# A mixture of experts with 608 static slots an expert in place of 640

## The chip, the core and the metric

The kernel runs on one core of a Trainium2 chip, in one launch. The time is the device time of that core in microseconds (us), from the start to the end of the program. Beside the timed runs one execution was taken by the hardware profiler; every duration in this document comes from that execution. TensorE (PE) multiplies, and its weight loads are recorded apart (PEld) because they run beside the products; VectorE (DVE), ScalarE (ACT) and GpSimd (POOL) do the elementwise work, and SyncE's queue (SP) issues most DMAs.

## What is computed

Attention with only the 32 largest scores of each row kept, then a feed-forward layer with a squared ReLU, then a mixture of eight experts of which each token uses two. Cut to the part that matters here:

```python
def _moe2_ref(x, w_gate, w_noise, noise, w1, w2):        # x: 2304 tokens of 512
    noisy_logits = x @ w_gate + np.log1p(np.exp(x @ w_noise)) * noise
    top2 = np.argpartition(-noisy_logits, 2, axis=1)[:, :2]
    top2_w = softmax of the two logits
    for e in range(8):
        for k in range(2):
            mask = top2[:, k] == e
            h = np.maximum(x[mask] @ w1[e], 0.0)          # 512 -> 1024
            out[mask] += top2_w[mask, k, None] * (h @ w2[e])
```

2304 tokens with two choices each make 4608 rows over eight experts, 576 on average. How many an expert gets depends on the data.

## The kernel before

Attention runs first, with the feed-forward layer and the routing of finished tokens as background work. The routing writes each token's row, with its two gate weights, its first expert and its token number in four more columns (`ROW` = 516), into the DRAM buffer `xs`, in which expert e owns the rows from e x 2304 on; `base` counts how many it has. The first `CAP` = 640 rows of each expert are its static slots: they have been filled with empty rows (`zero_fill`, by tiles of 128), and the code for them is laid out without a look at the counts. Rows beyond them go through a general path at the end (`over`, `extra`, `blank`, `beyond`), under a branch that is taken only when some expert has more than `CAP` rows.

The 640 slots are five tiles of 128, in two parts: columns 0 to 384 (three tiles) and 384 to 640 (two tiles), `PARTS`. `fetch` (L507) loads a tile of rows (`mr`, L514), turns it by four transposes on TensorE (L517) into a PSUM tile `ph`, and splits it into a high part on ACT (L521) and a low part on DVE (L522), both fp32r, `xe`; `gate` works out the gate weight and the token number on POOL (`info`).

`expert` (L529) first gathers the current output rows (`cur`, L539, an indirect DMA). Then it goes over eight blocks f of 128 hidden units. A block loads its weights (`raww`, L559, three buffers), splits them into high and low on ACT (L563) and DVE (L564) as `wi` and `wo`, and for each part makes 12 products into `ph` (L570 to L572: four slices of the 512 inputs, high x high, high x low, low x high), with the part's columns moving. ReLU (ACT, L576) and the low rest (DVE, L577) give `ht`. One block later `second` makes three products a tile (L551 to L553) with 128 columns of `ht` as weights and the 512 columns of `wo` moving, and adds over the blocks in the tile's bank `acc` (three banks, two more named `acc2`). After the last block DVE makes `y` = `acc` x gate + `cur` (L591, three buffers) and POOL writes it by token number (L592, an indirect DMA).

The first parts of experts 0 and 1 (`EARLY`) run earlier, beside the last feed-forward work; their second parts follow alone, and then experts 2 to 7 with both parts. While an expert runs, the next one's tiles are fetched, one a block. `ph` has two buffers, so a block's first product waits until DVE has read the block before last. The order on each engine comes from a scheduler that goes by priorities and by modelled times; nothing of it is written by hand.

Of the kernel before, what the change touches and what calls it, by code (L numbers as in the profile page):

```python
# [8 lines left out]
F32 = mybir.dt.float32  # L9
F32R = mybir.dt.float32r  # L10
I32 = mybir.dt.int32
# [3 lines left out]
ALU = mybir.AluOpType  # L15
PSUM = bass.MemoryType.PSUM

P = 128
# [34 lines left out]
def attention_ffn_moe(ctx: ExitStack, tc: tile.TileContext, q, k, v, w_ffn, w_route, noise, w_exp, out,  # L53
# [3 lines left out]
    nc = tc.nc  # L57
    B, H, S, D = SHAPE
    NT, DM = out.shape
# [4 lines left out]
    NFE = F // P  # L64
    NC = DM // P
# [3 lines left out]
    SCALE = 1.0 / float(D) ** 0.5  # L69
    CH = 384  # L70
    CT = CH // P
    CAP = 640
    CAPT = CAP // P
    PARTS = [(0, 384), (384, CAP - 384)]
    ROW = DM + 4

# [3 lines left out]
    xs = nc.dram_tensor(f"xs{tag}", (E * NT, ROW), F32, kind="Internal").ap()  # L80
# [3 lines left out]
    ident = cpool.tile([P, P], F32, name="ident")  # L84
# [19 lines left out]
    for t, (b, i) in enumerate(tiles):  # L104
        if i == 0:
            nc.gpsimd.iota(tok_i[:, t:t + NFULL], pattern=[[P, NFULL]], base=b * S, channel_multiplier=1)
        elif i is None:
            nc.gpsimd.iota(tok_i[:, t:t + 1], pattern=[[0, 1]], base=b * S + NFULL * P, channel_multiplier=1)
            nc.gpsimd.tensor_scalar(tok_i[LEFT:P, t:t + 1], tok_i[LEFT:P, t:t + 1], 1.0, float(S - LEFT),
                                    op0=ALU.mult, op1=ALU.add)  # L110
# [387 lines left out]
    def gate(gi, xr, e):  # L498
        nc.gpsimd.tensor_scalar(gi[:, 0:1], xr[:, DM + 2:DM + 3], float(e), xr[:, DM:DM + 1],  # L499
                                op0=ALU.is_equal, op1=ALU.mult)  # L500
        nc.gpsimd.tensor_scalar(gi[:, 1:2], xr[:, DM + 2:DM + 3], float(e), None, op0=ALU.is_equal)  # L501
        nc.gpsimd.tensor_scalar(gi[:, 1:2], gi[:, 1:2], -1.0, 1.0, op0=ALU.mult, op1=ALU.add)
        nc.gpsimd.tensor_tensor(gi[:, 1:2], gi[:, 1:2], xr[:, DM + 1:DM + 2], op=ALU.mult)
        nc.gpsimd.tensor_tensor(gi[:, 2:3], gi[:, 0:1], gi[:, 1:2], op=ALU.add)
        nc.gpsimd.tensor_copy(gi[:, 3:4].bitcast(I32), xr[:, DM + 3:DM + 4].bitcast(I32))

    def fetch(e, parts):  # L507

        xe = [mpool.tile([P, 2, NC, n], F32R, name=f"xe{o}") for o, n in parts]
        t0, t1 = parts[0][0] // P, sum(parts[-1]) // P  # L510
        info = mpool.tile([P, CAPT, 4], F32, name="info")
        for t in range(t0, t1):
            xr = mpool.tile([P, ROW], F32, name="mr", bufs=3)
            nc.sync.dma_start(xr, xs[e * NT + t * P:e * NT + (t + 1) * P, :])  # L514
            pt = ps_m.tile([P, DM], F32, name="ph")
            for c in range(NC):
                nc.tensor.transpose(pt[:, c * P:(c + 1) * P], xr[:, c * P:(c + 1) * P], ident)  # L517
            i, off = place(parts, t)
            hi, lo = xe[i][:, 0, :, off:off + P], xe[i][:, 1, :, off:off + P]
            pv = pt.rearrange("p (c s) -> p c s", c=NC)  # L520
            nc.scalar.activation(hi, pv, AF.Copy)  # L521
            nc.vector.tensor_tensor(lo, pv, hi.bitcast(F32), op=ALU.subtract)  # L522
            gate(info[:, t, :], xr, e)
            yield None
        yield xe, info

# [2 lines left out]
    def expert(e, parts, ahead):  # L529

        xe, info = found.pop(0)
        tiles_ = range(parts[0][0] // P, sum(parts[-1]) // P)
        cur = {}
        for t in tiles_:
            cu = cur[t] = mpool.tile([P, DM], F32, name="cur", bufs=6)
            if cleared[0] < 6:
                nc.gpsimd.memset(cu, 0.0)
                cleared[0] += 1
            nc.gpsimd.indirect_dma_start(  # L539
                out=cu, out_offset=None, in_=out,  # L540
                in_offset=bass.IndirectOffsetOnAxis(ap=info[:, t, 3:4].bitcast(I32), axis=0),
                bounds_check=NT - 1, oob_is_err=False)
        acc = {}
        for n, t in enumerate(tiles_):
            acc[t] = ps_acc.tile([P, DM], F32, name="acc") if n < 3 else ps_m.tile([P, DM], F32, name="acc2")

        def second(f, wo, hs):
            for t in tiles_:
                i, off = place(parts, t)
                sl = slice(off, off + P)  # L550
                nc.tensor.matmul(acc[t], hs[i][:, 0, sl], wo[:, 0, :], start=(f == 0), stop=False)  # L551
                nc.tensor.matmul(acc[t], hs[i][:, 0, sl], wo[:, 1, :], start=False, stop=False)  # L552
                nc.tensor.matmul(acc[t], hs[i][:, 1, sl], wo[:, 0, :], start=False, stop=(f == NFE - 1))  # L553
                yield True, 0.5

        prev = None
        for f in range(NFE):
            raw = mpool.tile([P, 2, DM], F32, name="raww", bufs=3)
            nc.sync.dma_start(raw, w_exp[e, f])  # L559
            wi = fpool.tile([P, 2, DM], F32R, name="wi", bufs=2)  # L560
            wo = fpool.tile([P, 2, DM], F32R, name="wo", bufs=2)
            for i, w in enumerate((wi, wo)):
                nc.scalar.activation(w[:, 0, :], raw[:, i, :], AF.Copy)  # L563
                nc.vector.tensor_tensor(w[:, 1, :], raw[:, i, :], w[:, 0, :].bitcast(F32), op=ALU.subtract)  # L564
            hs = []
            for i, (o, n) in enumerate(parts):
                ph = ps_m.tile([P, DM], F32, name="ph")
                for c in range(NC):
                    sl = slice(c * P, (c + 1) * P)
                    nc.tensor.matmul(ph[:, 0:n], wi[:, 0, sl], xe[i][:, 0, c, :], start=(c == 0), stop=False)  # L570
                    nc.tensor.matmul(ph[:, 0:n], wi[:, 0, sl], xe[i][:, 1, c, :], start=False, stop=False)  # L571
                    nc.tensor.matmul(ph[:, 0:n], wi[:, 1, sl], xe[i][:, 0, c, :], start=False, stop=(c == NC - 1))  # L572
                    if c < NC - 1:
                        yield True, 0.5
                ht = mpool.tile([P, 2, n], F32R, name=f"ht{o}")
                nc.scalar.activation(ht[:, 0, :], ph[:, 0:n], AF.Relu)  # L576
                nc.vector.scalar_tensor_tensor(ht[:, 1, :], ph[:, 0:n], 0.0, ht[:, 0, :].bitcast(F32),  # L577
                                               op0=ALU.max, op1=ALU.subtract)
                hs.append(ht)
                yield True, 0.5  # L580
            if prev is not None:
                yield from second(*prev)
            prev = (f, wo, hs)
            if f >= 1:
                x = next(ahead, None)
                if x is not None:
                    found.append(x)
        yield from second(*prev)
        for t in tiles_:
            y = mpool.tile([P, DM], F32, name="y", bufs=3)  # L590
            nc.vector.scalar_tensor_tensor(y, acc[t], info[:, t, 2:3], cur[t], op0=ALU.mult, op1=ALU.add)  # L591
            apart(row_writes.setdefault(e, []), nc.gpsimd.indirect_dma_start(  # L592
                out=out, out_offset=bass.IndirectOffsetOnAxis(ap=info[:, t, 3:4].bitcast(I32), axis=0),
                in_=y, in_offset=None, bounds_check=NT - 1, oob_is_err=False),
                "the slots of an expert hold different tokens")

    found = []
# [66 lines left out]
    chunks, t = [], 0  # L664
# [140 lines left out]
    opool = ctx.enter_context(tc.tile_pool(name="opool", bufs=1))  # L805
# [18 lines left out]
    def blank(e, row, rows):  # L824

        taken = opool.tile([P, 1], F32, name="inside")
        nc.vector.tensor_tensor(taken, row, base[:, e:e + 1], op=ALU.is_lt)
        nc.vector.tensor_scalar(taken, taken, float(E * NT), None, op0=ALU.mult)
        at = opool.tile([P, 1], I32, name="at")
        nc.vector.tensor_tensor(at, taken, row, op=ALU.add)  # L830
        nc.vector.tensor_scalar(row, row, float(P), None, op0=ALU.add)
        nc.gpsimd.indirect_dma_start(
            out=xs, out_offset=bass.IndirectOffsetOnAxis(ap=at, axis=0), in_=rows, in_offset=None,
            bounds_check=E * NT - 1, oob_is_err=False)
# [43 lines left out]
    with tc.If(any_extra > 0):  # L878
        none = mpool.tile([P, ROW], F32, name="mr", bufs=3)
        nc.gpsimd.memset(none, 0.0)  # L880
        nc.vector.tensor_copy(none[:, DM + 3:DM + 4].bitcast(I32), far)
        row = opool.tile([P, 1], F32, name="row")
        for e in range(E):
            nc.vector.tensor_scalar(row, first, float(e * NT), None, op0=ALU.add)
            with tc.For_i(0, (NT - CAP) // P, 1):
                blank(e, row, none)
        for e in range(E):
            nc.vector.tensor_scalar(row, first, float(e * NT), None, op0=ALU.add)
            n_extra = nc.values_load(extra[0:1, e:e + 1], min_val=0, max_val=(NT - CAP + P - 1) // P)
            with tc.For_i(0, n_extra, 1):  # L890
                beyond(e, row)
# [82 lines left out]
```

## Time and profile before

| | us |
|---|---|
| median of 3 runs (1445.23 to 1450.17) | 1448.94 |
| the profiled execution | 1446.42 |
| its span, first to last instruction | 1444.6 |
| TensorE busy | 1271.8 (88%) |
| DVE, ACT, POOL busy | 941.0, 844.5, 818.4 |

The expert stage stands at the end of the span: its first products start at 941 us, experts 0 and 1 finish at 1080, and each later one takes about 58 us up to 1425. A busy time is the sum of recorded durations with overlaps counted once, and the end of a product is modelled; what products cost is therefore read from the distance between their starts.

### The profile page before, as it was taken

To read this page: it belongs to the slowest core of one execution; us is meant where nothing else is said; L and a number is where in the kernel's file an instruction comes from. 1 tells how busy PE (TensorE), PEld (TensorE's weight loads), DVE (VectorE), ACT (ScalarE), POOL (GpSimd) and SP (SyncE) were. 2 spreads that over 40 slices of the span, in tenths; PEclk is the share of its full clock that TensorE was granted. 3 is DMA by queue.
4 is the path that set the end of the run, shared out by engine and by line. 5 is a ranking of instruction groups with operands and counts; after the bars stand their busy time and mean duration, and the time that the engine had idled before them with its cause. 6 is when DMAs were issued, how large, how long until landed. Compare 5 with 4: busy or idle time off the path is not lost. (4 is left out here: it accounts for less than half of the span.)

```text
span 1444.6 us, 26379 instructions
## 1 busy us (share of the span) xinstructions
PE 1271.8 (88%) x7937; PEld 1089.4 (75%) x7937; DVE 941.0 (65%) x4944; ACT 844.5 (58%) x1741; POOL 818.4 (57%) x1446
## 2 busy tenths in 40 slices
PE   2566669877699999999999989899899999999995
PEld 1444558665588888878888878788778999999984
DVE  7989999999798489789999100145563434444431
ACT  4677788888687579678788534344453333333320
POOL 4778899888788558748866532615233315134121
PEclk9886679999799999999999999999999999999997
DMA  9964358564436635644632576846564434344231
GB/s 325 365 236 146 129 186 296 183 222 168 157 116 207 228 124 175 220 133 161 218 134 90 194 269 217 270 127 218 191 216 143 144 111 159 121 143 151 86 116 39
DMA packets 85251, 257.60 MB, mean 178 GB/s; under 512 B 10716, under 2 KB 10844, under 8 KB 85088
## 3 DMA queue, kind: packets, MB, share of 16 engines
q1 hardware_dynamic: 75808, 227.32, 47.3%
q0 software_dynamic: 9280, 28.40, 5.5%
q8 instruction: 67, 1.10, 0.3%
q14 instruction: 96, 0.79, 0.2%
HBM read 205.71 MB, written 52.06 MB: 178 GB/s over the span
## 5 line engine op out<-in xcount | busy, mean ns | idle before, releaser
L394 POOL TENSOR_TENSOR sb<-sb,w 128x576 f32<-128x576 f32 x144 | 206.5, 1441 | 23.5 <-ACT w L393 19.8
L367 DVE MATCH_REPLACE8 w<-m,sb 128x96 f32<-128x96 f32 x864 | 201.3, 242 | 0.0
L366 DVE MAX8 m<-sb 128x8 f32<-128x96 f32 x864 | 167.7, 245 | 31.4 <-ACT sb L358 25.7
L592 POOL DMA_INDIRECT out<-y,info x40 | 45.1, 1126 | 244.2 <-DVE y L591 237.6
L576 ACT ACTIVATE ht<-ph 128x384 fp32r<-128x384 f32 (+1 forms) x128 | 56.0, 437 | 215.0 <-PE ph L572 200.2
L577 DVE SCALAR_TENSOR_TENSOR ht<-ph,ht 128x384 fp32r<-128x384 f32 (+1 forms) x128 | 62.6, 489 | 180.2 <-ACT ht L576 161.0
L355 PE MATMUL ps<-K,qt 128*128 128x288 f32 x640 | 133.9, 336 | 41.6 <-ACT sb L358 17.2
L570 PE MATMUL ph<-xe,wi 128*128 128x384 f32 (+1 forms) x512 | 159.5, 312 | 2.8 <-DVE xe L522 2.0
L571 PE MATMUL ph<-xe,wi 128*128 128x384 f32 (+1 forms) x512 | 159.5, 311 | 0.8 <-DVE xe L522 0.8
L572 PE MATMUL ph<-xe,wi 128*128 128x384 f32 (+1 forms) x512 | 158.9, 310 | 0.2 <-DVE wi L564 0.2
L355 PEld LDWEIGHTS ps<-K,qt 128*128 128x128 f32 x640 | 104.4, 210 | 56.4 <-ACT sb L358 24.0
L295 POOL TENSOR_TENSOR gt<-r,gt 128x384 fp32r<-128x384 f32 x96 | 97.7, 1018 | 76.0 <-ACT gt L294 70.5
L406 PE MATMUL pa<-ident,sb 128*128 128x128 f32 x576 | 101.6, 302 | 38.0 <-DVE x L415 14.7
L393 ACT ACTIVATE w<-sb,keep 128x576 f32<-128x576 f32 x144 | 109.6, 772 | 36.2 <-POOL keep L389 35.3
L551 PE MATMUL acc<-wo,ht 128*128 128x512 f32 x320 | 126.7, 398 | 1.8 <-ACT ht L576 1.0
L552 PE MATMUL acc<-wo,ht 128*128 128x512 f32 x320 | 125.4, 394 | 0.0
L395 ACT ACTIVATE sb<-sb,keep 128x576 f32<-128x576 f32 x144 | 111.7, 776 | 22.1 <-POOL sb L394 21.2
L285 PE MATMUL pf<-xT,wi 128*128 128x384 f32 x320 | 113.8, 356 | 11.0 <-DMA wi<-wsc 8.5
L271 PE MATMUL acc<-wo,gt 128*128 128x512 f32 x288 | 117.4, 418 | 5.7 <-DMA wo<-wsc 3.0
L406 PEld LDWEIGHTS pa<-ident,sb 128*128 128x128 f32 x576 | 69.9, 151 | 62.2 <-issue 20.0
L286 PE MATMUL pf<-xT,wi 128*128 128x384 f32 x320 | 110.5, 345 | 3.6 <-POOL xT L421 3.6
L272 PE MATMUL acc<-wo,gt 128*128 128x512 f32 x288 | 112.8, 403 | 0.0
(180 smaller groups left out, 3530.4 us busy)
## 6 DMA issues: line engine op xcount, KB each, us to landing
wi<-wsc SPq DMA_DIRECT2D x96, 512.0 KB
wo<-wsc SPq DMA_DIRECT2D x96, 512.0 KB
raww<-in_exp SPq DMA_DIRECT2D x80, 512.0 KB
raw<-in_ffn SPq DMA_DIRECT2D x32, 512.0 KB
wsc<-csp SPq DMA_DIRECT2D x32, 512.0 KB
xs<-xr SPq DMA_DIRECT2D x40, 258.0 KB
mr<-xs SPq DMA_DIRECT2D x40, 258.0 KB
qn<-in_q SPq DMA_DIRECT2D x40, 256.0 KB
```

The source lines that it names most:

```text
L271: nc.tensor.matmul(acc[tt], gt[:, 0, sl], wo[:, 0, :], start=(f == 0), stop=False)
L285: nc.tensor.matmul(ph[:, 0:n], wi[:, 0, sl], xT[:, 0, c, 0:n], start=(c == 0), stop=False)
L355: nc.tensor.matmul(ps[:, n, 0:HS], st, kt[:, n * HS:(n + 1) * HS], start=(i == 0), stop=(i == len(pairs) - 1))
L366: nc.vector.max(top, sb[:, sl])
L367: nc.vector.match_replace(out=w[:, sl], in_to_replace=top, in_values=sb[:, sl], imm_value=NEG)
L394: nc.gpsimd.tensor_tensor(sb, sb, w, op=ALU.subtract)
L406: nc.tensor.transpose(pt[:, c * P:(c + 1) * P], e[:, c * P:(c + 1) * P], ident)
L551: nc.tensor.matmul(acc[t], hs[i][:, 0, sl], wo[:, 0, :], start=(f == 0), stop=False)
L552: nc.tensor.matmul(acc[t], hs[i][:, 0, sl], wo[:, 1, :], start=False, stop=False)
L570: nc.tensor.matmul(ph[:, 0:n], wi[:, 0, sl], xe[i][:, 0, c, :], start=(c == 0), stop=False)
L571: nc.tensor.matmul(ph[:, 0:n], wi[:, 0, sl], xe[i][:, 1, c, :], start=False, stop=False)
L572: nc.tensor.matmul(ph[:, 0:n], wi[:, 1, sl], xe[i][:, 0, c, :], start=False, stop=(c == NC - 1))
```

## The change

`CAP` becomes 608, so the second part has 224 columns instead of 256, and the last tile 96 rows instead of 128. The tile loops round up, so there are still five tiles, and `zero_fill` still writes 640 rows an expert. The last tile's load, transposes, splits, gather, products of the second layer, `y` and write are cut to 96 rows. The general path begins at slot 608; its `blank` gets two more DVE operations that keep it from writing beyond the expert's own rows, since the rest is no longer a whole number of tiles.

```diff
-    CAP = 640
-    CAPT = CAP // P
+    CAP = 608
+    CAPT = -(-CAP // P)
     PARTS = [(0, 384), (384, CAP - 384)]
...
-        t0, t1 = parts[0][0] // P, sum(parts[-1]) // P
+        t0, t1 = parts[0][0] // P, -(-sum(parts[-1]) // P)
...
-            nc.sync.dma_start(xr, xs[e * NT + t * P:e * NT + (t + 1) * P, :])
+            n = min(P, CAP - t * P)
+            nc.sync.dma_start(xr[0:n], xs[e * NT + t * P:e * NT + t * P + n, :])
...
-                nc.tensor.transpose(pt[:, c * P:(c + 1) * P], xr[:, c * P:(c + 1) * P], ident)
+                nc.tensor.transpose(pt[:, c * P:c * P + n], xr[0:n, c * P:(c + 1) * P], ident[0:n, 0:n])
...
+        rows = {t: min(P, CAP - t * P) for t in tiles_}
...
-                out=cu, out_offset=None, in_=out,
-                in_offset=bass.IndirectOffsetOnAxis(ap=info[:, t, 3:4].bitcast(I32), axis=0),
+                out=cu[0:rows[t]], out_offset=None, in_=out,
+                in_offset=bass.IndirectOffsetOnAxis(ap=info[0:rows[t], t, 3:4].bitcast(I32), axis=0),
...
-                sl = slice(off, off + P)
-                nc.tensor.matmul(acc[t], hs[i][:, 0, sl], wo[:, 0, :], start=(f == 0), stop=False)
...
+                sl = slice(off, off + rows[t])
+                to = acc[t][0:rows[t]]
+                nc.tensor.matmul(to, hs[i][:, 0, sl], wo[:, 0, :], start=(f == 0), stop=False)
...
-            nc.vector.scalar_tensor_tensor(y, acc[t], info[:, t, 2:3], cur[t], op0=ALU.mult, op1=ALU.add)
+            n = rows[t]
+            nc.vector.scalar_tensor_tensor(y[0:n], acc[t][0:n], info[0:n, t, 2:3], cur[t][0:n],
+                                           op0=ALU.mult, op1=ALU.add)
...
+        outside = opool.tile([P, 1], F32, name="outside")
+        nc.vector.tensor_scalar(outside, row, float((e + 1) * NT), None, op0=ALU.is_ge)
+        nc.vector.tensor_tensor(taken, taken, outside, op=ALU.add)
...
-            with tc.For_i(0, (NT - CAP) // P, 1):
+            with tc.For_i(0, -(-(NT - CAP) // P), 1):
                 blank(e, row, none)
```

The scheduler's order of the attention and the feed-forward layer stays; in the expert stage it moves a few instructions at the change from one expert to the next. On DVE, at the change from expert 6 to 7 (the names with numbers: `acc_16599` and `acc_16600` are the fourth and fifth tile's banks of expert 6, `ht_17190` and `ht_17206` the two parts of expert 7's first block), before:

```order
L591 SCALAR_TENSOR_TENSOR y<-acc,info,cur 128x512 x3
L591 SCALAR_TENSOR_TENSOR y<-acc_16599,info,cur 128x512
L564 TENSOR_TENSOR wo<-raww,wo 128x512
L577 SCALAR_TENSOR_TENSOR ht_17190<-ph,ht_17190 128x384
L591 SCALAR_TENSOR_TENSOR y<-acc_16600,info,cur 128x512
L577 SCALAR_TENSOR_TENSOR ht_17206<-ph,ht_17206 128x256
```

The same place of the changed kernel, whose line numbers are three or four higher:

```order
L595 SCALAR_TENSOR_TENSOR y<-acc,info,cur 128x512 x3
L595 SCALAR_TENSOR_TENSOR y<-acc_16599,info,cur 128x512
L567 TENSOR_TENSOR wo<-raww,wo 128x512
L595 SCALAR_TENSOR_TENSOR y<-acc_16600,info,cur 96x512
L580 SCALAR_TENSOR_TENSOR ht_17190<-ph,ht_17190 128x384
L580 SCALAR_TENSOR_TENSOR ht_17206<-ph,ht_17206 128x224
```

The fifth `y` has moved ahead of the first `ht` of the next expert. On TensorE, in the first block of an expert (the same two banks, here of expert 6, and `xe_16128`, its first part), before:

```order
L552 MATMUL acc<-wo,ht_16622 128x512
L551 MATMUL acc_16599<-wo,ht_16638 128x512
L552 MATMUL acc_16599<-wo,ht_16638 128x512
L570 MATMUL ph<-xe_16128,wi 128x384
L571 MATMUL ph<-xe_16128,wi 128x384
```

The same place of the changed kernel:

```order
L555 MATMUL acc<-wo,ht_16622 128x512
L554 MATMUL acc_16599<-wo,ht_16638 128x512
L555 MATMUL acc_16599<-wo,ht_16638 128x512
L554 MATMUL acc_16600<-wo,ht_16638 96x512
L555 MATMUL acc_16600<-wo,ht_16638 96x512
L573 MATMUL ph<-xe_16128,wi 128x384
```

The fifth tile's first two products, which followed the next block's first layer, now stand ahead of it.

## Rows read from the trace of the kernel before

**Rows 1.** Engines' busy time, share of the span, instructions (the page).

```profile
PE 1271.8 (88%) x7937; PEld 1089.4 (75%) x7937; DVE 941.0 (65%) x4944; ACT 844.5 (58%) x1741; POOL 818.4 (57%) x1446
```

**Rows 2.** Busy time by stage, with granted clock, DMA share, GB/s: experts 0-1, 3, 4, tail.

```profile
core 0: us, PE busy (x) PEld busy (x) DVE busy (x) ACT busy (x) POOL busy (x), PEclk, DMA share, GB/s
...
1021.96:1080.35 58.39, 53.46 (x328) 46.57 (x329) 33.43 (x59) 27.14 (x55) 16.67 (x50) 0.97 0.63 207
...
1138.69:1197.05 58.36, 58.36 (x334) 52.77 (x333) 25.26 (x42) 18.82 (x38) 18.29 (x41) 1.00 0.42 134
1197.05:1255.38 58.33, 58.33 (x334) 52.73 (x334) 25.23 (x42) 18.81 (x38) 18.93 (x41) 1.00 0.43 135
...
1424.90:1444.60 19.70, 1.80 (x8) 1.12 (x6) 3.57 (x5) 0.00 (x0) 4.95 (x5) 0.60 0.21 69
```

**Rows 3.** Timeline of TensorE in expert 4: start, duration, what (in us).

```profile
1200.32 0.34 PE L570 MATMUL ph<-xe,wi 128*128 128x384 f32 x1
...
1202.43 0.86 PE L553 MATMUL acc<-wo,ht 128*128 128x512 f32 x3
...
1203.60 0.28 PE L570 MATMUL ph<-xe,wi 128*128 128x256 f32 x1
...
1205.02 0.62 PE L553 MATMUL acc<-wo,ht 128*128 128x512 f32 x2
1205.48 0.40 PE L551 MATMUL acc<-wo,ht 128*128 128x512 f32 x1
...
1206.87 0.60 PE L517 MATMUL ph<-ident,mr 128*128 128x128 f32 x4
1207.23 0.94 PE L553 MATMUL acc<-wo,ht 128*128 128x512 f32 x3
```

**Rows 4.** Timeline of the weight loads after a wait of TensorE, at two places.

```profile
600.65 0.19 PEld L271 LDWEIGHTS acc<-wo,gt 128*128 128x128 f32 x1 [0.17 <-issue]
600.75 0.19 PEld L272 LDWEIGHTS acc<-wo,gt 128*128 128x128 f32 x1
...
1041.53 0.19 PEld L570 LDWEIGHTS ph<-xe,wi 128*128 128x128 f32 x1 [1.15 <-ACT wi L563]
1041.64 0.19 PEld L571 LDWEIGHTS ph<-xe,wi 128*128 128x128 f32 x1
```

**Rows 5.** Waits from 1021.96 to 1080.35 (total us, times, longest).

```profile
ACT wi L563 <- DMA raww<-in_exp: 12.6, 8, 3.8
```

**Rows 6.** Plain fp32 products of the route: timeline, then all of them.

```profile
521.90 1.05 PE L180 MATMUL pf<-xt,wg 128*16 128x128 f32 x8
...
L180 PE MATMUL pf<-xt,wg 128*16 128x128 f32 x144 | 18.8, 274 | 0.0
```

**Rows 7.** Timeline of DVE and TensorE at two changes of experts.

```profile
1257.27 0.55 DVE L577 SCALAR_TENSOR_TENSOR ht<-ph,ht 128x384 fp32r<-128x384 f32 x1
1257.73 0.74 DVE L591 SCALAR_TENSOR_TENSOR y<-acc,info,cur 128x512 f32<-128x512 f32 x1
...
1258.64 0.34 PE L570 MATMUL ph<-xe,wi 128*128 128x384 f32 x1
...
1373.79 0.75 DVE L591 SCALAR_TENSOR_TENSOR y<-acc,info,cur 128x512 f32<-128x512 f32 x1 [3.60 <-PE ph L572]
...
1375.06 0.55 DVE L577 SCALAR_TENSOR_TENSOR ht<-ph,ht 128x384 fp32r<-128x384 f32 x1
...
1375.12 0.39 PE L552 MATMUL acc<-wo,ht 128*128 128x512 f32 x1
1375.66 0.44 PE L570 MATMUL ph<-xe,wi 128*128 128x384 f32 x1
```

**Rows 8.** The end of the chain that ended last.

```profile
1424.94 0.76 DVE y L591
...
1432.95 0.80 POOL out L592
```

**Rows 9.** POOL's indirect DMA of the output rows, all of them.

```profile
L592 POOL DMA_INDIRECT out<-y,info x40 | 45.1, 1126 | 244.2 <-DVE y L591 237.6 <-issue 5.7 <-DVE ht L577 0.6
```

More of the change, by code (lines that the diff above doesn't have):

```diff
@@ L513, in fetch @@
             xr = mpool.tile([P, ROW], F32, name="mr", bufs=3)
-            nc.sync.dma_start(xr, xs[e * NT + t * P:e * NT + (t + 1) * P, :])
+            n = min(P, CAP - t * P)
+            nc.sync.dma_start(xr[0:n], xs[e * NT + t * P:e * NT + t * P + n, :])
             pt = ps_m.tile([P, DM], F32, name="ph")
             for c in range(NC):
-                nc.tensor.transpose(pt[:, c * P:(c + 1) * P], xr[:, c * P:(c + 1) * P], ident)
+                nc.tensor.transpose(pt[:, c * P:c * P + n], xr[0:n, c * P:(c + 1) * P], ident[0:n, 0:n])
             i, off = place(parts, t)
-            hi, lo = xe[i][:, 0, :, off:off + P], xe[i][:, 1, :, off:off + P]
-            pv = pt.rearrange("p (c s) -> p c s", c=NC)
+            hi, lo = xe[i][:, 0, :, off:off + n], xe[i][:, 1, :, off:off + n]
+            pv = pt.rearrange("p (c s) -> p c s", c=NC)[:, :, 0:n]
             nc.scalar.activation(hi, pv, AF.Copy)
             nc.vector.tensor_tensor(lo, pv, hi.bitcast(F32), op=ALU.subtract)
-            gate(info[:, t, :], xr, e)
+            gate(info[0:n, t, :], xr[0:n], e)
             yield None
@@ L531, in expert @@
         xe, info = found.pop(0)
-        tiles_ = range(parts[0][0] // P, sum(parts[-1]) // P)
+        tiles_ = range(parts[0][0] // P, -(-sum(parts[-1]) // P))
+        rows = {t: min(P, CAP - t * P) for t in tiles_}
         cur = {}
@@ L549, in second @@
                 i, off = place(parts, t)
-                sl = slice(off, off + P)
-                nc.tensor.matmul(acc[t], hs[i][:, 0, sl], wo[:, 0, :], start=(f == 0), stop=False)
-                nc.tensor.matmul(acc[t], hs[i][:, 0, sl], wo[:, 1, :], start=False, stop=False)
-                nc.tensor.matmul(acc[t], hs[i][:, 1, sl], wo[:, 0, :], start=False, stop=(f == NFE - 1))
+                sl = slice(off, off + rows[t])
+                to = acc[t][0:rows[t]]
+                nc.tensor.matmul(to, hs[i][:, 0, sl], wo[:, 0, :], start=(f == 0), stop=False)
+                nc.tensor.matmul(to, hs[i][:, 0, sl], wo[:, 1, :], start=False, stop=False)
+                nc.tensor.matmul(to, hs[i][:, 1, sl], wo[:, 0, :], start=False, stop=(f == NFE - 1))
                 yield True, 0.5
@@ L590, in expert @@
             y = mpool.tile([P, DM], F32, name="y", bufs=3)
-            nc.vector.scalar_tensor_tensor(y, acc[t], info[:, t, 2:3], cur[t], op0=ALU.mult, op1=ALU.add)
+            n = rows[t]
+            nc.vector.scalar_tensor_tensor(y[0:n], acc[t][0:n], info[0:n, t, 2:3], cur[t][0:n],
+                                           op0=ALU.mult, op1=ALU.add)
             apart(row_writes.setdefault(e, []), nc.gpsimd.indirect_dma_start(
-                out=out, out_offset=bass.IndirectOffsetOnAxis(ap=info[:, t, 3:4].bitcast(I32), axis=0),
-                in_=y, in_offset=None, bounds_check=NT - 1, oob_is_err=False),
+                out=out, out_offset=bass.IndirectOffsetOnAxis(ap=info[0:n, t, 3:4].bitcast(I32), axis=0),
+                in_=y[0:n], in_offset=None, bounds_check=NT - 1, oob_is_err=False),
                 "the slots of an expert hold different tokens")
```

## The prediction, made before the changed kernel had run

> **What bounds the kernel now.** I read the page's busy shares first, then the stages, then the spacing of the products inside one stage. Over the whole span TensorE is the busiest engine, at 88% [rows 1], but what the change touches is only the expert stage, and there the stages' table decides [rows 2]. [...]
>
> The recorded duration of a product (0.28 us for 256 columns) is a latency and overlaps the next one; its cost is the distance to the next start. In [rows 3] twelve products of 256 columns run from 1203.60 to the start of L553 at 1205.02: 1.42 us, 118 ns each. Twelve of 384 columns run from 1200.32 to 1202.43: 176 ns each. Six of 512 run from 1205.48 to 1206.87: 232 ns each. The three lie on one line, about 0.445 ns a column plus 4 ns. One block f of a full expert is 12 x 176 + 12 x 118 + 15 x 232 ns = 7.0 us; eight of them and 20 transposes (four in 0.36 us, [rows 3]) give 56.1 + 1.8 = 57.9 us of the 58.35. The sum closes, so a nanosecond taken from a product there is taken from the time.
>
> **The change, part by part.** *Products of the first layer.* The second part has 12 products a block, eight blocks, eight experts: 768 of them go from 256 to 224 columns. No fp32r product under 256 columns stands in this trace, so the cost at 224 has to be bounded. On the line of the three sizes it is 118 - 32 x 0.445 = 104 ns. But each product also brings its own weights, and where a product has waited and the next load is not held back by a running product, the loads show their own pace: 600.65 to 600.75, and 1041.53 to 1041.64 [rows 4], 0.10 to 0.11 us a load of 128 fp32r columns. Loads of the next weights run beside the current product, so a product cannot be closer to the next than a load takes. At 256 columns (118 ns) the load is just covered; at 224 (104 ns) it would not be. I take 110 ns, the load, because it is a measured duration of the operation that these very products issue: a saving of 8.3 ns, where the column count alone would give 14.3.
>
> [...]
>
> Per full expert: 96 x 8.3 ns = 0.80 us, and over six experts 4.8 us. Bounds for these: 0 (if changing weights costs the 8 ns that lie between 110 and 118) and 96 x 14.3 x 6 = 8.2 us.
>
> *Transposes of the last tile.* Four of 128 columns take 0.36 us [rows 3]; with 96 I take them in proportion, 0.27. Five of the last tiles are transposed inside full experts (those of 3 to 7): 0.45 us, between 0 and that.
>
> *Products of the second layer.* The last tile's load weights of 96 columns instead of 128, but they still move 512 columns: 232 ns, with the load under it. No gain, and no reason for a loss.
>
> *Experts 0 and 1.* The same 2 x 0.80 us, plus 0.2 for transposes, is freed, but weights that land late set part of this stretch [rows 2, 5]. Between 0 and 1.8; I take half, 0.9 us.
>
> *DMAs, ACT, DVE, POOL.* One load of rows, one gather of `cur` and one write of `out` an expert carry 96 rows instead of 128; relu and rest handle 224 columns instead of 256. In full experts this lies beside TensorE, with ACT and DVE idle for more than half [rows 2]; at experts 0 and 1 it is inside the half above. At the end, one `out` write of five is shorter. The tail from the last `y` (1424.94) to the end is 19.7 us, a chain of `y` and POOL's writes [rows 2, 8], and its length is set by the waits, not the rows: 0, at most a few tenths. The three new DVE lines of `blank` lie in the branch that isn't taken; nothing.
>
> *What moves.* At the change of experts DVE now makes the fifth `y` ahead of the first `ht` of the new expert, and TensorE takes the last tile's two products before the next block's first layer instead of after. Queued behind that `y` is an `ht` that frees the `ph` buffer of the next block. At the usual change of experts `ht` ended at 1257.82 and TensorE took the buffer at 1258.64 [rows 7]: 0.8 us of cover, of which the `y` (0.74) eats most, while two more products (0.46) in front on TensorE give some back. That hides it. At the last change of experts the cover is gone already: the fourth `y` came after 3.60 us in which DVE was idle, `ht` ended at 1375.61 and TensorE started at 1375.66 behind it, after some 0.3 us idle [rows 7]. There the fifth `y` ends at about 1375.8, where TensorE would want its bank at 1375.35, and the two products follow; net about 0.3 us more. I add 0.3, between 0 and 5 x 0.74 = 3.7 us if all five changes looked like that one.
>
> **The sum.** 4.8 + 0.45 + 0.9 - 0.3 = 5.9 us less. Against the profiled execution, which took 1446.42 us with a span of 1444.6, that is 1440.5; it was 2.5 us under the median of the three runs, 1448.94. On the median the forecast is **1443.0 us**, 0.41% less. About 0.3% (4.3 us) is what a measurement of this kernel can tell from no change, so the forecast lies only 1.6 us beyond it.
>
> **The rivals.**
> (1) *No floor: the line of the column counts goes on.* For it: 256, 384 and 512 lie on one line [rows 3], with no bend. Against: the loads' own pace [rows 4]. Then 8.2 + 0.45 + 1.5 (half of 2 x 1.37 + 0.2) - 0.3 = 9.8 less: 1439.1. [...]
> (2) *The floor lies higher.* If a load under a running product cannot repeat faster than the 118 ns seen at 256 columns, the products gain nothing. Only the transposes remain, and the stall: 0.45 + 0.1 - 0.3, 1448.7. Against: three sizes on one line make 118 look like columns, not a floor.
> (3) *Slower: fp32r keeps its one-pass rate only down to 256 columns.* The trace shows the plain fp32 form of the same engine at the route's products: 144 records for 72 products, two each, eight records in 1.05 us of which the last lasts 0.27 [rows 6], 111 ns a record of 128 columns, 1.74 ns a column. If the 224-column form fell to that it would take 389 ns, 271 more, times 768: 208 us more, 1657. For it: nothing under 256 was run in fp32r. Against: all sizes seen are one record a product on one line, and the built program still has one matmul a product at 224. [...]
> (4) *The change of experts stalls.* If the fifth `y` is late at all five changes, 3.7 instead of 0.3: 2.5 less, 1446.4.
> (5) *An expert overflows 608 slots.* Worked out from the reference's own inputs, the eight experts get 579, 592, 562, 540, 583, 585, 576 and 591 tokens, so 16 slots are left. If it did, the general path would run 8 x 14 rounds of `blank`, each with an indirect DMA of 1.13 us on POOL [rows 9]: over 126 us more.
>
> **How the numbers follow.** Forecast 0.68, (1) 0.12, (2) 0.08, (3) 0.06, (4) 0.05, (5) 0.01. The three runs before span 1445.2 to 1450.2, so a median may be off by some 2 us either way; of the forecast's 0.68 I give 0.49 to a gain over 0.3% and 0.19 to one within it. Faster: 0.49 + 0.12 = 0.61. Same: 0.19 + 0.08 + 0.04, 0.31. Slower: 0.08, with (3), (5) and 0.01 of scatter. The range goes from just under (1), 1438, to just under (2), 1448.5; (3), (5) and half of (2) lie outside.
>
> **What would show it.** The twelve 224-column products of a block should lie 110 ns apart, with weight loads at the same pace: 104 would show (1), 118 (2), near 390 (3). A full expert should take 57.5 us instead of 58.35. The weight waits of experts 0 and 1 should grow a little. At the changes of experts no idle over half a microsecond on TensorE, except the one that was late before. No line of the general path should appear. I am wrong if the spacing is not between 104 and 118 ns, or if TensorE idles inside full experts.

## The result

The changed kernel is slower. Its median is 1454.21 us (7 runs, 1450.71 to 1459.24) against 1445.47 for the kernel before (7 runs, 1444.12 to 1450.17), a ratio of 1.0054 with a 95% interval of 1.0032 to 1.0076: 8.7 us more where 5.9 less had been forecast. The profiled execution took 1452.72 us with a span of 1450.9, 6.3 more than that of before.

### The profile page after: what moved, and what is told of

Its sections match the earlier page's. It is cut to its first block, busy times and chain, and to the rows that moved or that the text cites. A ratio compares the mean times of both kernels' runs of the same rounds, so it can differ in the third digit from the quotient of the medians.

```text
span 1450.9 us, 26379 instructions
## 1 busy us (share of the span) xinstructions
PE 1266.9 (87%) x7937; PEld 1080.6 (74%) x7937; DVE 937.6 (65%) x4944; ACT 843.1 (58%) x1741; POOL 819.8 (57%) x1446
## 3 DMA queue, kind: packets, MB, share of 16 engines
q0 software_dynamic: 9024, 28.39, 5.4%
## 5 line engine op out<-in xcount | busy, mean ns | idle before, releaser
L554 PE MATMUL acc<-wo,ht 128*128 128x512 f32 (+1 forms) x320 | 127.0, 399 | 3.5 <-ACT ht L579 2.1
L555 PE MATMUL acc<-wo,ht 128*128 128x512 f32 (+1 forms) x320 | 125.5, 395 | 0.0
L285 PE MATMUL pf<-xT,wi 128*128 128x384 f32 x320 | 113.1, 353 | 12.7 <-DMA wi<-wsc 9.3
L406 PEld LDWEIGHTS pa<-ident,sb 128*128 128x128 f32 x576 | 70.2, 151 | 56.9 <-issue 18.6
```

The costliest lines, as they stand in the source:

```text
L285: nc.tensor.matmul(ph[:, 0:n], wi[:, 0, sl], xT[:, 0, c, 0:n], start=(c == 0), stop=False)
L406: nc.tensor.transpose(pt[:, c * P:(c + 1) * P], e[:, c * P:(c + 1) * P], ident)
L554: nc.tensor.matmul(to, hs[i][:, 0, sl], wo[:, 0, :], start=(f == 0), stop=False)
L555: nc.tensor.matmul(to, hs[i][:, 0, sl], wo[:, 1, :], start=False, stop=False)
```

## The profile after

On TensorE the forecast came true. Its busy time fell from 1271.8 us [rows 1] to this (the page's engines: busy, share of the span, instructions):

```profile
PE 1266.9 (87%) x7937; PEld 1080.6 (74%) x7937; DVE 937.6 (65%) x4944; ACT 843.1 (58%) x1741; POOL 819.8 (57%) x1446
```

The timeline of TensorE in expert 4 of the changed kernel, start and duration, shows the first two and the last of the twelve products of 224 columns and what follows them. It answers [rows 3]:

```profile
1200.21 0.27 PE L573 MATMUL ph<-xe,wi 128*128 128x224 f32 x1
1200.31 0.28 PE L574 MATMUL ph<-xe,wi 128*128 128x224 f32 x1
...
1201.43 0.27 PE L575 MATMUL ph<-xe,wi 128*128 128x224 f32 x1
1201.54 0.63 PE L556 MATMUL acc<-wo,ht 128*128 128x512 f32 x2
```

From the first start, 1200.21, to the start of L556 at 1201.54 are 1.33 us for the twelve, 111 ns each, where 256 columns had 118 by the same count. The weight loads beside them (same view, PEld) have the same pace within the rounding, from 1200.32 to 1201.33 nine steps of 112 ns:

```profile
1200.32 0.19 PEld L575 LDWEIGHTS ph<-xe,wi 128*128 128x128 f32 x1
1200.43 0.19 PEld L573 LDWEIGHTS ph<-xe,wi 128*128 128x128 f32 x1
...
1201.33 0.19 PEld L575 LDWEIGHTS ph<-xe,wi 128*128 128x128 f32 x1
```

The stages of the changed kernel (columns as in [rows 2]), of which the first is that of experts 0 and 1, the second one full expert, the third the last 20 us:

```profile
1017.80:1078.80 61.00, 54.91 (x328) 46.82 (x329) 32.52 (x59) 26.49 (x55) 17.32 (x50) 0.92 0.60 198
...
1196.30:1253.80 57.50, 57.50 (x334) 51.35 (x333) 24.67 (x42) 18.69 (x37) 18.20 (x40) 1.00 0.43 136
...
1430.50:1450.90 20.40, 0.00 (x0) 0.00 (x0) 0.00 (x0) 0.00 (x0) 0.00 (x0) 0.50 0.01 2
```

A full expert takes 57.5 us instead of 58.35, TensorE busy throughout. The loss stands in the third row. The last product starts at 1419.9 us, 6.4 earlier than before, but the end comes 31.0 us after it, where it came after 18.3: 12.7 us more. In the last 20.4 us no engine computes and the DMAs move 2 GB/s, so no large transfer is under way.

What runs there are instructions of POOL's sequencer (POOLq), which the busy time leaves out. The view by line shows them: durations as shortest/middle/longest in ns, then first and last start. L886 and L920 are the branches `tc.If(any_extra > 0)` and `tc.If(again > 0)`, and L914 is the line that opens the program's context, to which its end is put down. Of the changed kernel:

```profile
L886 POOLq INC_SWDGE_SEM  x1: 2508/2508/2508, 1432.0 to 1432.0; - x1
L920 POOLq INC_SWDGE_SEM  x1: 2477/2477/2477, 1438.0 to 1438.0; - x1
L914 POOLq DRAIN  x3: 46/107/9550, 1440.5 to 1450.6; - x3
```

The same three of the kernel before, whose lines are L878, L912 and L906:

```profile
L878 POOLq INC_SWDGE_SEM  x1: 388/388/388, 1438.6 to 1438.6; - x1
L912 POOLq INC_SWDGE_SEM  x1: 357/357/357, 1442.5 to 1442.5; - x1
L906 POOLq DRAIN  x3: 40/107/898, 1442.9 to 1444.3; - x3
```

The two increments at the branches take 2.1 us more each, and the drain 8.65 us more: together 12.9 us, which accounts for the 12.7. The rest of the difference between the two profiled executions, 6.4 us the other way: what runs ahead of the stretch of experts 0 and 1 ended 4.2 us earlier (a second trace of before, e9 below, reaches that point at 1017.7 us, as early as the changed kernel, so before scatters by as much by itself); the stretch itself took 2.6 us longer; the six full experts up to the last product 4.8 less.

One more row differs. The timeline of POOL at the third of the five last writes, with the idle time ahead of it in brackets, first before and then after:

```profile
1429.74 0.98 POOL L592 DMA_INDIRECT out<-y,info  x1 [1.45 <-issue]
```

```profile
1422.26 0.97 POOL L597 DMA_INDIRECT out<-y,info  x1 [0.30 <-issue]
```

Before, POOL paused 1.15 us there for nothing that the trace names; after, it didn't.

## The experiments

Three theories could explain the longer end, and the expectations go by their letters. **A**: the form with 96 rows makes the increments and the drain dear. **B**: POOL keeps something for every indirect DMA that it has issued, clears it when a total passes a mark (the pause in before), and what isn't cleared by the end is paid for there; with 16 indirect DMAs of 96 rows instead of 128 the total stays under the mark. **C**: the code of the general path, which the change alters too. Before issues 116 indirect DMAs with 14,848 rows in all, after 116 with 14,336. A time below that stands without an interval is that of one run, the profiled one.

**The form of the DMAs alone, both ways.** e1 is the changed kernel with the last tile's gather and write at 128 rows again, the 32 rows without a token pointing nowhere. e3 is the kernel before, 640 slots, with these DMAs and `y` at 96 rows.

```diff
 (e1, against the changed kernel)
+            if n < P:
+                nc.gpsimd.tensor_copy(info[n:P, t, 3:4].bitcast(I32), nowhere[n:P])
...
-                out=cu[0:rows[t]], out_offset=None, in_=out,
-                in_offset=bass.IndirectOffsetOnAxis(ap=info[0:rows[t], t, 3:4].bitcast(I32), axis=0),
+                out=cu, out_offset=None, in_=out,
+                in_offset=bass.IndirectOffsetOnAxis(ap=info[:, t, 3:4].bitcast(I32), axis=0),
...
+            if n < P:
+                nc.gpsimd.memset(y[n:P], 0.0)
...
 (e3, against the kernel before)
-                out=cu, out_offset=None, in_=out,
-                in_offset=bass.IndirectOffsetOnAxis(ap=info[:, t, 3:4].bitcast(I32), axis=0),
+                out=cu[0:min(P, 608 - t * P)], out_offset=None, in_=out,
+                in_offset=bass.IndirectOffsetOnAxis(ap=info[0:min(P, 608 - t * P), t, 3:4].bitcast(I32), axis=0),
...
```

> The changed kernel with one thing undone: the last tile's gather and write carry 128 rows again (the rows 96 to 127 hold a token number out of range and are skipped), while products, transposes, loads and the first-layer columns stay at 608 slots. In the changed kernel TensorE ended 6.4 us earlier than before, but POOL's two semaphore increments of its indirect DMAs took 2.51 and 2.48 us instead of 0.39 and 0.36 and its DRAIN 9.55 instead of 0.90 us. Theory A, the 96-row form of the indirect DMAs makes that end: increments back under 0.5 us each, DRAIN about 0.9 us, and the time 6 us under the kernel before, about 1439 us. Theory B, the end depends on how many rows all indirect DMAs together have carried (14,848 before, 14,336 after): here 14,848 again, so the same short end, 1439 us. Theory C, the end comes from the changed code of the general path: the end stays long, about 1452 us.

> The kernel before, 640 slots, with the last tile's gather and write cut to 96 rows (the slots from 608 on hold no token with these inputs); the products stay at 256 columns and 128 rows. Theory A (the 96-row form): increments 2.5 us each and DRAIN about 9.5 us, time 12 to 13 us above the kernel before. Theory B (the total of rows): the total is that of the changed kernel, so the same long end. Theory C (code of the general path): the end stays as before, DRAIN 0.9 us.

e3 took 1458.74 us beside 1448.0 for before, with the changed kernel's end to the nanosecond, by the same view:

```profile
L880 POOLq INC_SWDGE_SEM  x1: 2508/2508/2508, 1438.1 to 1438.1; - x1
L914 POOLq INC_SWDGE_SEM  x1: 2477/2477/2477, 1444.1 to 1444.1; - x1
L908 POOLq DRAIN  x3: 46/107/9550, 1446.6 to 1456.7; - x3
```

e1 has the short end:

```profile
L892 POOLq INC_SWDGE_SEM  x1: 388/388/388, 1441.4 to 1441.4; - x1
...
L920 POOLq DRAIN  x3: 40/107/898, 1446.0 to 1447.5; - x3
```

Its time was 1449.25 us (10 runs) against 1448.0 (13 runs), ratio 1.0003 (0.9986 to 1.0021). The end is repaired, but the 1439 us expected were missed by 10. Its stretch of experts 0 and 1 took 65.4 us at a granted clock of 0.90; whether the copies and fills that e1 adds on POOL have to do with that was not tested. Since e3 has the general path of before and e1 that of after, C falls. A and B are both left.

**More DMAs of 128 rows, the 96-row ones kept; fewer, with none of 96 rows.** e2 adds two indirect gathers of 128 rows into a spare tile to the changed kernel, ahead of the second parts (`own` holds the row numbers 0 to 127). e4 leaves the three gathers of expert 0's first part out of the kernel before; the buffers are zeroed in any case.

```diff
 (e2, against the changed kernel)
+    spare = mpool.tile([P, NTT * E], F32, name="spare", bufs=1)
+    for _ in range(2):
+        nc.gpsimd.indirect_dma_start(
+            out=spare, out_offset=None, in_=noise.rearrange("p t e -> p (t e)"),
+            in_offset=bass.IndirectOffsetOnAxis(ap=own, axis=0), bounds_check=P - 1, oob_is_err=False)
 (e4, against the kernel before)
+            if e == 0 and t < 3:
+                continue
```

> The changed kernel with two more indirect DMAs of 128 rows (gathers of the noise into a tile that nobody reads) ahead of the second parts of the experts. Theory A (the 96-row form): the end stays long, increments 2.5 us each and DRAIN about 9.5 us, time about 1452. Theory B (the total of rows or descriptors, with a boundary between after and before): 14,592 rows; the end may turn short if the boundary lies under that, DRAIN about 0.9 us and time about 1440; a DRAIN that changes by more than 1 us at all speaks for B. Theory C: long, as A.

> The kernel before without three of its 116 indirect DMAs: the gathers of the first part of expert 0, whose rows of the output are still zero, as its cleared tiles are. All indirect DMAs have 128 rows, 14,464 in all. Theory A (the 96-row form): the end as before, increments under 0.5 us, DRAIN 0.9 us, time as before within 2 us. Theory B (the total, with a boundary between 14,336 and 14,848): the end may turn long, DRAIN toward 9.5 us and the time 10 us or more up; a DRAIN that changes by more than 1 us speaks for B. Theory C: as before.

This is the pair that decides. e4 does less work than before, has no DMA of 96 rows, and took 1457.56 us beside 1448.0:

```profile
L880 POOLq INC_SWDGE_SEM  x1: 2448/2448/2448, 1436.7 to 1436.7; - x1
...
L908 POOLq DRAIN  x3: 40/107/9310, 1445.1 to 1455.0; - x3
```

e2 does more than the changed kernel, keeps all sixteen DMAs of 96 rows, and took 1448.03, some 8 more than expected but with the short end:

```profile
L894 POOLq INC_SWDGE_SEM  x1: 348/348/348, 1440.3 to 1440.3; - x1
...
L922 POOLq DRAIN  x3: 46/107/730, 1444.7 to 1446.0; - x3
```

A falls: the form with 96 rows is not needed for the long end, and it does not suffice for it. What decides is how much has been issued.

**Where the mark lies, and what the rest costs.** In the program e5 has the two added gathers at the start of expert 4, and e7 only one of them; e6 adds 24 at the same place to the kernel before.

```diff
 (e5; e7 has 1 for 2)
+        for _ in range(2 if e == 4 else 0):
+            nc.gpsimd.indirect_dma_start(
+                out=spare, out_offset=None, in_=noise.rearrange("p t e -> p (t e)"),
+                in_offset=bass.IndirectOffsetOnAxis(ap=own, axis=0), bounds_check=P - 1, oob_is_err=False)
```

> The changed kernel with two more indirect DMAs of 128 rows (gathers of the noise that nobody reads) at the start of expert 4, where POOL is idle for two thirds of the time. [...] Then what TensorE gained stays: 4 to 5 us under the kernel before, ratio about 0.997. If the gain of the full experts is eaten in the stretch of experts 0 and 1 (theory D: the narrower second parts or the new order make that stretch 3 to 7 us longer), the ratio is 0.999 to 1.002.

> [...]

> The kernel before with 24 more indirect DMAs of 128 rows at the start of expert 4. Theory B: the list is cleared 24 DMAs earlier, so about 34 instead of 10 are left at the end: increments about 0.87 and 0.84 us, DRAIN about 2.8 us. Theory A (96-row form): the end as before, 0.39, 0.36 and 0.90.

The scheduler did not leave the gathers at expert 4. In e5 they run beside the feed-forward layer, where those of e2 run too (837.2 to 846.3 us), so e5 repeats e2 with more runs, and not another place:

```profile
L809 POOL DMA_INDIRECT spare<-in_noise,own x2: 1027/1050/1074, 837.2 to 844.9; - x2
```

One more gather leaves the end long: e7 took 1457.63 us beside 1443.18 for before.

```profile
L893 POOLq INC_SWDGE_SEM  x1: 2528/2528/2528, 1436.9 to 1436.9; - x1
...
L921 POOLq DRAIN  x3: 46/107/9632, 1445.4 to 1455.6; - x3
```

Two make it short:

```profile
L893 POOLq INC_SWDGE_SEM  x1: 348/348/348, 1430.8 to 1430.8; - x1
...
L921 POOLq DRAIN  x3: 46/107/730, 1435.4 to 1436.7; - x3
```

With these two, e5 took 1441.39 us (12 runs) against 1443.18 (17 runs), ratio 0.9984 (0.9967 to 1.0002). It does all that the changed kernel does and two gathers more, and the 8.7 us are gone. e6 took 1485.88 us; its 24 gathers run from 840 to 947 us, the feed-forward layer ended 27 us later, and only its end can be read:

```profile
L885 POOLq INC_SWDGE_SEM  x1: 875/875/875, 1474.7 to 1474.7; - x1
...
L913 POOLq DRAIN  x3: 40/107/2858, 1480.0 to 1483.4; - x3
```

Side by side, with the count left at the end taken as all DMAs where nothing was cleared:

| kernel | indirect DMAs | rows | first increment, ns | drain, ns | left, worked out |
|---|---|---|---|---|---|
| e4 | 113 | 14,464 | 2448 | 9310 | 113 |
| after, e3 | 116 | 14,336 | 2508 | 9550 | 116 |
| e7 | 117 | 14,464 | 2528 | 9632 | 117 |
| e2, e5 | 118 | 14,592 | 348 | 730 | 8 |
| before | 116 | 14,848 | 388 | 898 | 10 |
| e6 | 140 | 17,920 | 875 | 2858 | 34 |

The first three give 20 ns a DMA in the increment (2448 to 2508 for three), so 188 + 20 x n; by that the last three had 8, 10 and about 34 left. The drain then has to follow without another choice: from 898 at 10 to 9550 at 116 it is 81.6 ns a DMA, which gives 735 at 8 (measured 730), 2856 at 34 (2858), 9305 at 113 (9310) and 9632 at 117 (9632). It is the number of DMAs and not their rows that sets these durations: e4 and e7 have the same rows and differ, and e8 below, with 116 DMAs and 14,080 rows, has 2508 and 9550 again.

The mark itself isn't a number of DMAs, since before with 116 passes it and e7 with 117 does not. In rows it lies between 14,464 and 14,592. In before and in e6 the 114th DMA brings the total to 114 x 128 = 14,592, with two and 26 still to come, and in e2 and e5 the 118th, the last, does. The 10, 34 and 8 left are then eight and those issued later, in all three. That it is rows that are counted, and not something that goes with them, is not shown. The pages count 9280 packets in the software queue for the 116 DMAs of before and 9024 for those of after, 256 less for 512 rows less, which makes an estimate of 80 packets for a DMA of 128 rows and 64 for one of 96. By this e7 stays at 9104 and before comes to 9120 at its 114th DMA, so a mark between these fits as well, and no kernel here separates the two.

The pause does not go with every clearing. It stands ahead of the 114th DMA in before, in its second trace e9 and in e1 (1.45, 1.45 and 1.44 us), and in e5 and e2 2.50 and 2.27 us for which the trace names no wait stand ahead of the 118th, where the last write of before and of e7 has 0.30. But in e6 nothing is seen at the 114th, nor at the 118th of e11 below (0.32 us):

```profile
1305.96 1.00 POOL L541 DMA_INDIRECT cur<-out,info  x1 [0.31 <-issue]
```

What POOL does in the pause is not known.

**How much of the gain is there, and how narrow is worth it.** e8 goes to 592 slots, 208 columns and 80 rows. e9 and e10 are second traces of before and after.

```diff
 (e8, against the changed kernel)
-    CAP = 608
+    CAP = 592
```

> 592 slots: second parts of 208 columns, a last tile of 80 rows (the largest expert has 592 tokens). If the weight load sets the distance of the narrow products, it stays at 111 ns and a full expert at 57.4 us; if the columns set it, about 97 to 104 ns and 56.2 to 56.8 us an expert. [...]

> The kernel before once more, for a second trace. It asks whether the stretch of experts 0 and 1 (58.4 us in the first trace, granted clock 0.97) scatters by itself. Theory S (scatter: late weights and the clock's fall after them): somewhere from 58 to 62 us, longer where the clock is lower. Theory D (the narrower parts make it longer): 58.4 within 0.5. The end as in the first trace: increments 0.39 and 0.36, DRAIN 0.90 us.

> The changed kernel once more. Its stretch of experts 0 and 1 took 61.0 us at a clock of 0.92. Theory S: 58 to 62 again, by the clock. Theory D: 61.0 within 0.5 or longer. Full experts 57.5 us, end as in its first trace: increments 2.51 and 2.48, DRAIN 9.55 us.

In e8 the products of 208 columns stand hardly closer than those of 224; the first and the last of a block, eleven steps, 110 ns each:

```profile
1198.06 0.26 PE L573 MATMUL ph<-xe,wi 128*128 128x208 f32 x1
...
1199.27 0.28 PE L575 MATMUL ph<-xe,wi 128*128 128x208 f32 x1
```

Its full experts take 57.4 to 57.5 us, as with 224 columns. Its end is the long one, its time 1449.55 us beside 1443.18. e9 took 1442.93 us with the short end, e10 1459.42 beside 1445.09 with the long one, and full experts again at 57.5. In e10 the stretch of experts 0 and 1 is this (stage row; then the longest wait of ACT in it: us in all, times, longest), and below the same of e5. The weights are waited for about as long in all, but the longest single wait is 5.9 us against 4.0:

```profile
1022.80:1085.80 63.00, 54.33 (x329) 46.41 (x330) 32.67 (x59) 26.80 (x55) 17.78 (x50) 0.92 0.61 192
...
ACT wi L566 <- DMA raww<-in_exp: 12.6, 6, 5.9
```

```profile
1017.60:1077.00 59.40, 52.48 (x329) 44.39 (x330) 32.56 (x60) 26.37 (x55) 17.79 (x50) 0.97 0.66 202
...
ACT wi L568 <- DMA raww<-in_exp: 13.3, 8, 4.0
```

**A version that is faster than both.** At the end of e5 and of before, DVE's last `y` wait for one of three buffers to be written out. e11 is e5 with five (the general path's `y`, which doesn't run, gets five too).

```diff
 (e11, against e5)
-            y = mpool.tile([P, DM], F32, name="y", bufs=3)
+            y = mpool.tile([P, DM], F32, name="y", bufs=5)
...
```

> The kernel of e5 (608 slots, two more indirect DMAs at expert 4) with five buffers for y instead of three. At the end, and at each change of experts, the fourth y waited for the first write of the output to land (4.9 us at the end of the kernel before, 4.2 in the changed one). If the wait goes and POOL's writes set the pace, about 1.3 us each, the end is some 3 us shorter than in e5, and the ratio to the kernel before is about 0.996; the short end of POOL stays (0.35, 0.32 and 0.73 us). If the last write's landing sets the end whatever the buffers, the ratio is that of e5, 0.998.

e11 took 1438.99 us (12 runs) against 1445.09 (17 runs), ratio 0.9962 (0.9944 to 0.9981), the only kernel here whose interval lies below 1. The last write of e5 and of e11, by POOL's timeline:

```profile
1426.03 0.95 POOL L599 DMA_INDIRECT out<-y,info  x1 [2.50 <-issue]
```

```profile
1423.52 0.95 POOL L599 DMA_INDIRECT out<-y,info  x1 [0.32 <-issue]
```

The end comes 16.2 us after the last product instead of 18.6. What five buffers alone would give the kernel before was not run, so how much of the 6.1 us comes from the narrower slots stays open.

## Why the prediction was wrong

**The tail: the step that failed.** It held that the last 19.7 us are "a chain of `y` and POOL's writes", "set by the waits, not the rows: 0, at most a few tenths". Up to the last write that is right, 8.9 us from the last product to the end of the last write before and 8.3 after. But the chain of [rows 8] breaks off there: the last write of before ends at 1435.2 us, with 9.4 us of the span still to go, and the prediction priced those as a constant. In them stand two increments and a drain of POOL, whose length hangs on what has been issued, and cutting 512 rows out of the program's indirect DMAs kept the total under the mark: +12.7 us. No rival had it; the slower one was looked for on TensorE, where the change is. What could have warned were the 9.4 us in which no engine is busy.

**Products of the first layer: right.** 110 ns was forecast with the weight load as the floor, and 111 measured, loads and products at one pace. Rival (1), 104, falls, and again with 208 columns in e8 (110); rivals (2) and (3) fall with their 118 and 390 too, and 256 columns mark no limit here. What carried the floor is the loads' own pace in the trace of before, 0.10 to 0.11 us [rows 4]. A full expert was to take 57.5 us and does; products and transposes together were to give 5.25 us in the six full experts, and 57.5 against 58.35 gives 5.1.

**The change of experts: right in size.** Only the last change stalls. Between the fourth tile's second product and the fifth tile's first, TensorE (timeline, idle in brackets) waits for the `y` that DVE ended late:

```profile
1369.09 0.74 DVE L595 SCALAR_TENSOR_TENSOR y<-acc,info,cur 96x512 f32<-96x512 f32 x1
```

```profile
1369.88 0.47 PE L554 MATMUL acc<-wo,ht 128*96 128x512 f32 x1 [0.37 <-DVE y L595]
```

From the product at 1369.12 to this one are 0.76 us where 0.23 is usual, 0.5 lost, beside some 0.3 that were lost at this change before: 0.2 more, where 0.3 was added. At the other four changes TensorE waits for nothing; rival (4) falls.

**Experts 0 and 1: wrong in sign, cause open.** 0.9 us less was taken, as half of what is freed. The stretch took 58.4, 59.7 and 59.3 us in before, e9 and e4, and 61.0, 63.0, 60.9, 59.4, 60.9, 62.9 and 63.4 in after, e10, e2, e5, e7, e11 and e8. Freeing TensorE did not shorten it, as a stretch that waits for weights allows. The weight waits did not grow either, as the prediction held they would: 10.2 us in after against 12.6 [rows 5]. The longer stretches go with a lower granted clock, 0.97 to 1.00 under 60 us, 0.92 to 0.94 from 61 to 63, 0.90 in e1's 65.4. All four over 62 us (e1, e8, e10, e11) have a single wait for weights of 5.0 to 7.3 us; of the others only e2 (5.8) has one over 4.0. But e3, with the products of before, has 61.0 at 0.94 too, and e5 59.4 at 0.97 with the narrow ones. Whether the change, its new order on the engines or the scatter of single executions makes it was not settled. Put at about 2 us, it gives with the 5.1 less and the 12.7 more a sum of 9.6 us, beside the 8.7 measured.

**The rest.** No line of the general path ran, and no expert overflowed 608 slots: rival (5) falls. With the end repaired (e5) the change is worth 1.8 us, with an interval that includes no change, and without room for the forecast's 5.9 (0.9959), so that would not have been reached with the short end either. The 0.9 that was taken for the stretch of experts 0 and 1, and did not show, is the likeliest part of what is missing; this was not shown.

## What to carry to other kernels

Follow the span to its last nanosecond: where the chain of work ends before the span does, read the sequencer's rows of the engines there, and don't price that time as a constant: here 512 rows less in the indirect DMAs made three instructions there 12.9 us longer. The changed kernel, with 116 indirect DMAs, lay two of them short of the mark, and two more, beside the feed-forward layer, brought the drain from 9.55 us down to 0.73: a kernel whose end shows such durations is worth the same try. And before narrowing the moving side of a product, compare the distance between products with the pace of the weight loads: at 118 ns (256 columns) against 111 (224) only 6% were left to gain, and 208 columns, at 110, brought next to nothing more.

## What the runs showed of the hardware

- In the runs with the long end its durations grow with the indirect DMAs that POOL has issued: the two `INC_SWDGE_SEM` by 20 ns a DMA each (2448 and 2417 ns at 113 in e4, 2508 and 2477 at 116 in after, 2528 and 2497 at 117 in e7), the last `DRAIN` by about 82 ns (9310, 9550 and 9632). Before, with 116 too, has 388, 357 and 898, which by the fit above stands for 10 left; that the others were cleared is the author's reading, which no row of a trace names. The short end came once the total had passed a point between 14,464 and 14,592 rows (or what goes with them). By the same fit 106 DMAs no longer counted in before and in e6, 110 in e2 and e5; eight were left each time, beside those issued later.
- These durations are the same to the nanosecond in several executions and kernels with the same number left (2508, 2477 and 9550 in after, e3, e8 and e10; 388, 357 and 898 in before and e9, where e1 has 361 for the second), so one trace was enough to tell the two ends apart.
- Weight loads of 128 fp32r columns never came closer than 0.10 us in the rows shown; products of 224 and of 208 columns have nearly the same distance, 111 and 110 ns.
